# Fewer dummies, scale groups moved into half-done K steps, and spread layer-norm halves at the head of a DiT block

## The chip, the cores and the metric

The kernel runs on one core of one Trainium2 chip. The metric is the device time of one execution in microseconds (us), as the median of several runs. Besides, one execution per kernel is profiled; its span is about 1.8 us shorter than the time of the same run (245.3 against 247.12 for the kernel before), so spans are compared with spans and times with times.

A difference of 2% is the bar for "faster" or "slower".

## The reference

A diffusion-transformer block over x of 2 x 256 x 1152 in bf16. Only its start matters:

```python
mod = (_silu(c) @ w_mod).reshape(B, 6, 1, D)          # six modulation vectors per batch
shift_a, scale_a, gate_a, shift_m, scale_m, gate_m = [mod[:, i] for i in range(6)]
h = _layernorm(x, axis=-1) * (1 + scale_a) + shift_a
qkv = (h @ wqkv).reshape(B, N, 3, H, Dh)
# ... attention, wo, second modulated layer norm, two MLP matmuls with gelu
```

The kernel computes K before the shift is there: it multiplies the scaled norm (without shift) into w_k. (It may: a shift of k that is the same for all keys of a batch adds to each query's scores a constant, which softmax removes.)

## The kernel before

The parts that the change touches, with cuts marked. TensorE is PE here.

```python
def warm(n, dst):                       # fp32 dummies on zeros; one is two passes of 256 columns
    for _ in range(n):
        nc.tensor.matmul(dst[:, 0:T // 2], zeros32[:, 0:P], zeros32, start=True, stop=True)
# ... two dummies, transposition of c, silu, then:

def norm1(t, c0, c1):                   # VectorE: normalize columns c0..c1 of token tile t
    nc.vector.tensor_scalar(xns[t][:, c0:c1], x_sb[:, t, c0:c1], mv1[:, t, 0:1], rstd1[:, t:t + 1],
                            op0=ALU.subtract, op1=ALU.mult)

SGROUPS = [(0, 2), (2, 4), (4, 6), (6, 8), (8, 9)]
def scale_group(g):                     # 9 tiny matmuls (2 columns) per chunk; the add is returned
    k0, k1 = SGROUPS[g]
    pm = aux_tile([P, k1 - k0, B], "pm")
    for j in range(k0, k1):
        for k in range(KD):
            nc.tensor.matmul(pm[:, j - k0, :], w_scale_a[:, k, j * P:(j + 1) * P], sT[:, k, 0:B], ...)
    return lambda: nc.vector.tensor_scalar_add(scale_a[:, k0:k1, :], pm[:], 1.0)

def transpose_x(ks, ts): ...            # PE transposes chunks of xns into one PSUM tile pt

def modulate(pt, i, k, b, j0, eng):     # scale while copying out of PSUM, one batch at a time
    dst, src, sc = hT0[:, k, b * N:(b + 1) * N], pt[:, i, j0:j0 + N], scale_a[:, k, b:b + 1]
    if eng == "d": nc.vector.tensor_scalar_mul(dst, src, sc)
    else:          nc.scalar.mul(dst, src, sc)

def k_step(k, c0=0, c1=T):              # K chunk k into six PSUM accumulators
    for m in range(KM1):
        ...
        nc.tensor.matmul(pk[m][:, c0:c1], w_k[:, k, m * P:(m + 1) * P], hT0[:, k, c0:c1], ...)

def both(pt, k):                        # batch 0 on VectorE, batch 1 on ScalarE, same PSUM tile
    for b, e in enumerate("da"):
        modulate(pt, 0, k, b, b * N, e)

warm(13, pwarm)
# ... layer-norm statistics and first-half norms of the four tiles, scale group 0, k_steps 0 and 1 ...
modulate(pt_b, 0, 2, 0, 0, "d")
modulate(pt_b, 1, 3, 0, 0, "a")
for t in range(NT):                     # second-half norms, four in a row
    norm1(t, CUT, D)
k_step(1, N, T)
pt_d = transpose_x([2, 3], BT[1])
modulate(pt_d, 0, 2, 1, 0, "d")
modulate(pt_d, 1, 3, 1, 0, "a")
k_step(2, 0, N)
k_step(2, N, T)
scale_group(2)()
pt = transpose_x([4], range(NT))
both(pt, 4)
k_step(3)
pt = transpose_x([5], range(NT))
both(pt, 5)
k_step(4)
scale_group(3)()
# ... and so on to k_step(8), then three k panels, q, attention, MLP ...
```

Weights come over one DMA queue in the order of use: x, scale group 0, w_k rows 0 and 1, scale group 1, w_k rows 2 and 3, and so on.

Of the kernel before, what the change touches and what calls it, by code (L numbers as in the profile page):

```python
# [19 lines left out]
def kernel(  # L20
# [12 lines left out]
    B, N, D = x.shape  # L33
# [4 lines left out]
    T = B * N  # L38
    NT = T // P
# [20 lines left out]
    def acc_tile(shape, name, dt=FP32):  # L60
        return psum.tile(shape, dt, name=name, tag="acc", bufs=6)

    def aux_tile(shape, name, dt=FP32):
        return psum.tile(shape, dt, name=name, tag="aux", bufs=2)
# [34 lines left out]
    KM1 = 6  # L99
# [55 lines left out]
    pwarm = acc_tile([P, T], "pwarm")  # L155
# [4 lines left out]
    def warm(n, dst):  # L160
        for _ in range(n):
            nc.tensor.matmul(dst[:, 0:T // 2], zeros32[:, 0:P], zeros32, start=True, stop=True)  # L162
# [48 lines left out]
    def norm1(t, c0, c1):  # L211
        nc.vector.tensor_scalar(  # L212
            xns[t][:, c0:c1], x_sb[:, t, c0:c1], mv1[:, t, 0:1], rstd1[:, t:t + 1],
            op0=ALU.subtract, op1=ALU.mult,
        )
# [4 lines left out]
    def scale_group(g):  # L220
# [4 lines that stand above are left out]
                nc.tensor.matmul(  # L225
                    pm[:, j - k0, :], w_scale_a[:, k, j * P:(j + 1) * P], sT[:, k, 0:B],
                    start=(k == 0), stop=(k == KD - 1),
                )
        return lambda: nc.vector.tensor_scalar_add(scale_a[:, k0:k1, :], pm[:], 1.0)

    def transpose_x(ks, ts):
        pt = aux_tile([P, len(ks), len(ts) * P], "pt", BF16)
        for i, k in enumerate(ks):
            for j, t in enumerate(ts):
                nc.tensor.transpose(pt[:, i, j * P:(j + 1) * P], xns[t][:, k * P:(k + 1) * P], ident[:])  # L235
        return pt

    def modulate(pt, i, k, b, j0, eng):
        dst, src, sc = hT0[:, k, b * N:(b + 1) * N], pt[:, i, j0:j0 + N], scale_a[:, k, b:b + 1]
        if eng == "d":  # L240
            nc.vector.tensor_scalar_mul(dst, src, sc)  # L241
        else:
            nc.scalar.mul(dst, src, sc)

    pk = [None] * KD

    def k_step(k, c0=0, c1=T):
        for m in range(KM1):
            if k == 0 and c0 == 0:
                pk[m] = acc_tile([P, T], "pk")  # L250
            nc.tensor.matmul(  # L251
                pk[m][:, c0:c1], w_k[:, k, m * P:(m + 1) * P], hT0[:, k, c0:c1],
                start=(k == 0 and c0 == 0), stop=(k == KD - 1), skip_group_check=True,
            )
# [30 lines left out]
    CUT = 4 * P  # L285
    BT = [range(b * TPB, (b + 1) * TPB) for b in range(B)]

    def both(pt, k):
        for b, e in enumerate("da"):
            modulate(pt, 0, k, b, b * N, e)  # L290

    warm(13, pwarm)
    for j in range(NPD):
        stats_piece(0, j)
    sqrt1(0)
# [14 lines left out]
    add = scale_group(0)  # L310
# [8 lines left out]
    recip1(3)  # L319
    norm1(3, 0, CUT)  # L320
    k_step(0, 0, N)
    k_step(1, 0, N)
    pt_c = transpose_x([0, 1], BT[1])
    modulate(pt_c, 0, 0, 1, 0, "d")
    modulate(pt_c, 1, 1, 1, 0, "a")
    add = scale_group(1)
    k_step(0, N, T)
    pt_b = transpose_x([2, 3], BT[0])
    add()
    modulate(pt_b, 0, 2, 0, 0, "d")  # L330
    modulate(pt_b, 1, 3, 0, 0, "a")
    for t in range(NT):
        norm1(t, CUT, D)
    k_step(1, N, T)
    pt_d = transpose_x([2, 3], BT[1])
    modulate(pt_d, 0, 2, 1, 0, "d")
    modulate(pt_d, 1, 3, 1, 0, "a")
    k_step(2, 0, N)
    k_step(2, N, T)
    scale_group(2)()  # L340
    pt = transpose_x([4], range(NT))
    both(pt, 4)
    k_step(3)
    pt = transpose_x([5], range(NT))
    both(pt, 5)
    k_step(4)
    scale_group(3)()
    pt = transpose_x([6], range(NT))
    both(pt, 6)
    k_step(5)  # L350
    pt = transpose_x([7], range(NT))
    both(pt, 7)
    k_step(6)
    scale_group(4)()
    pt = transpose_x([8], range(NT))
    both(pt, 8)
    k_step(7)
    k_step(8)
    for m in range(KM1):
        k_evac(m)  # L360
# [344 lines left out]
    for b in range(B):  # L705
        for stepped in (True, False):
# [3 lines left out]
            for m, k in steps:  # L710
                m0 = m - m % 2
# [94 lines left out]
```

## Time and profile before

| kernel before | |
|---|---|
| time, median of the first 3 runs | 246.26 us (246.14 to 246.86) |
| span of the profiled execution (that run: 247.12 us) | 245.3 us |
| PE busy | 239.3 us, 98% |
| dummies end, first w_scale_a matmul | 11.04 us |
| k panels start | 28.42 us |

The chain that ended last, shares by engine, from the page of the kernel before:

```profile
PE 97%; DVE 1%; ACT 0%; issue 0%; DVEq 0%
```

So time is won only where PE itself waits or does work nobody needs. Both are found in the first 28 us. The timeline of PE shows the head; columns are start, length, engine, line, operation, tiles, shapes, count, and in brackets the idle time before and what ended it. Kernel before:

```profile
1.19 2.08 PE L162 MATMUL pwarm<-zeros 128*128 128x256 f32 x4 [1.19 <-DVE eps_t L93]
3.20 0.19 PE L165 MATMUL pc<-ident,c_sb 18*128 18x18 bf16 x1
3.32 7.88 PE L162 MATMUL pwarm<-zeros 128*128 128x256 f32 x26
11.04 0.59 PE L225 MATMUL pm<-sT,w_scale_a 128*128 128x2 bf16 x18
...
17.75 0.81 PE L251 MATMUL pk<-big,w_k 128*128 128x256 bf16 x6 [0.59 <-DVE big L241]
...
18.86 0.38 PE L235 MATMUL pt<-ident,xn 128*128 128x128 bf16 x4
19.08 1.46 PE L251 MATMUL pk<-big,w_k 128*128 128x512 bf16 x6
20.37 0.39 PE L235 MATMUL pt<-ident,xn 128*128 128x128 bf16 x4
20.60 1.46 PE L251 MATMUL pk<-big,w_k 128*128 128x512 bf16 x6
...
28.42 4.05 PE L280 MATMUL pk<-big,w_k 128*128 128x512 bf16 x18
```

A record is longer than the distance to the next start (512 columns: 0.379 us against 0.216; I call the excess the drain), so work is read from start to start: a k_step of 512 columns takes 20.37 - 19.08 = 1.29 us. The dummies run without a break to 11.04 us. After the dummies, the idle 0.59 us at 17.75 is the only wait of PE for VectorE (0.75 us from start to start). Its cause is in VectorE's timeline of the kernel before: four norms in a row ahead of the modulation that k_step 2 needs.

```profile
15.93 1.51 DVE L212 TENSOR_SCALAR xn<-x_sb,mv,rstd 128x640 bf16<-128x640 bf16 x4
17.36 0.34 DVE L241 TENSOR_SCALAR big<-pt,scale_a 128x256 bf16<-128x256 bf16 x1
```

One more line, from the table of waits before (us in total, times, longest): ScalarE's modulations wait for VectorE's modulation of the same PSUM tile, eight times.

```profile
ACT big L243 <- DVE big L241: 10.2, 8, 1.6
```

No ScalarE modulation overlaps its VectorE partner: each of the eight starts 0.03 to 0.04 us after the partner has ended (19.30 + 0.35 = 19.65, then 19.69).

Not in a page view, but in the single records of the trace: the dummies' passes (26 of them for the thirteen dummies) start every 0.427 us up to 7.3 us and every 0.216 us after. The clock record puts the change at 7.42 us. I call this the opening of the gate, and the rates before and after the half and the full or open clock.

### The profile page before, as it was taken

The page shows a single profiled execution, that of the slowest core. Times are in us where ns is not written, and L with a number is a line of the kernel's source. Part 1 is how long each engine was busy: PE and PEld are TensorE (multiplying, and loading weights), DVE is VectorE, ACT ScalarE, POOL GpSimd, SP SyncE. Part 2 cuts the span into 40 slices and gives each one's busy share as a digit, 9 for nine tenths or more (in the row PEclk, how much of TensorE's full clock was granted, in tenths as well). Part 3 has the DMA queues.
Part 4 walks back from the last instruction along what each step waited for, and adds up shares of the span by engine and source line. Part 5 has one row for each costly group of instructions (what it writes and reads, how often), then busy time and mean ns, then how long its engine had stood idle before and what let it go on. Part 6 is the DMA issues. An engine that isn't in the chain of part 4 may idle for free.

```text
span 245.3 us, 3997 instructions
## 1 busy us (share of the span) xinstructions
PE 239.3 (98%) x1708; PEld 147.0 (60%) x1708; DVE 92.9 (38%) x200; ACT 61.4 (25%) x119; POOL 25.4 (10%) x37
## 2 busy tenths in 40 slices
PE   8989999999999999999999999999999999999993
PEld 5776444457667656788854444444566556655673
DVE  4662452324614578933000999970010000000001
ACT  6432432225414321564333222332000000000000
POOL 1000000022000222200000000001112211111111
PEclk9999999999999999999999999999999999999999
DMA  6999999993679997248999999199630000000000
GB/s 214 328 315 326 379 370 392 390 391 136 167 234 397 390 377 116 48 90 276 391 391 391 351 327 319 25 332 329 202 105 19 17 16 16 19 17 30 20 16 16
DMA packets 48780, 53.28 MB, mean 217 GB/s; under 512 B 9587, under 2 KB 36475, under 8 KB 48763
## 3 DMA queue, kind: packets, MB, share of 16 engines
q1 hardware_dynamic: 41312, 50.14, 61.1%
q10 hardware_dynamic: 6939, 1.71, 4.3%
q0 software_dynamic: 512, 1.19, 1.6%
q8 instruction: 13, 0.21, 0.4%
q14 instruction: 4, 0.03, 0.0%
HBM read 50.14 MB, written 1.19 MB: 209 GB/s over the span
## 4 chain that ended last, share of the span: by engine, by line
PE 97%; DVE 1%; ACT 0%; issue 0%; DVEq 0%
PE pacc L695 29%; PE pacc L751 29%; PE pacc L641 7%; PE pq L472 7%; PE pacc L551 7%; PE pk L251 4%; PE pwarm L162 4%; PE pk L280 2%; PE pa L589 2%; PE ps_s L509 2%; PE pn L370 2%; PE pm L225 1%; PE pt L235 1%; DVE xn L212 1%; PE pg L452 0%; DVE big L241 0%
## 5 line engine op out<-in xcount | busy, mean ns | idle before, releaser
L695 PE MATMUL pacc<-hT,w_f 128*128 128x256 bf16 (+1 forms) x432 | 70.5, 326 | 0.0
L751 PE MATMUL pacc<-w_f,gT 128*128 128x384 bf16 (+2 forms) x468 | 70.5, 314 | 0.0
L751 PEld LDWEIGHTS <-gT 128*128 128x128 bf16 x468 | 44.3, 98 | 26.3
L695 PEld LDWEIGHTS <-w_f 128*128 128x128 bf16 x432 | 42.1, 98 | 27.7
L757 DVE TENSOR_TENSOR tmp<-pacc,gate 128x384 f32<-128x384 f32 (+2 forms) x13 | 6.9, 527 | 65.6 <-PE pacc L751 55.1
L727 ACT ACTIVATE gT<-pacc 128x512 bf16<-128x512 f32 x24 | 14.3, 597 | 32.7 <-PE pacc L695 32.7
L423 DVE SCALAR_TENSOR_TENSOR part<-w_gate_m,s,part 128x1152 f32<-128x1152 bf16 x16 | 21.4, 1414 | 0.0
L641 PE MATMUL pacc<-w_o,big 128*128 128x384 bf16 x108 | 18.1, 326 | 0.0
L472 PE MATMUL pq<-hT,w_q 128*128 128x512 bf16 x81 | 18.0, 380 | 0.0
L551 PE MATMUL pacc<-w_v,hT 128*128 128x384 bf16 x108 | 17.7, 326 | 0.0
L759 POOL TENSOR_TENSOR o_sb<-tmp,x 128x384 bf16<-128x384 f32 (+1 forms) x12 | 11.6, 970 | 51.9 <-DVE tmp L757 51.9
L551 PEld LDWEIGHTS <-hT 128*128 128x128 bf16 x108 | 10.5, 98 | 7.1 <-issue 0.2
L641 PEld LDWEIGHTS <-big 128*128 128x128 bf16 x108 | 10.3, 98 | 7.3 <-issue 0.7
L251 PE MATMUL pk<-big,w_k 128*128 128x256 bf16 (+1 forms) x72 | 13.3, 326 | 1.2 <-DVE big L241 0.6
L472 PEld LDWEIGHTS <-w_q 128*128 128x128 bf16 x81 | 7.8, 98 | 9.4 <-issue 0.3
L162 PE MATMUL pwarm<-zeros 128*128 128x256 f32 x30 | 10.0, 502 | 1.2 <-DVE eps_t L93 1.2
L647 POOL TENSOR_TENSOR x<-tmp,x_sb 128x384 f32<-128x384 f32 x8 | 7.3, 913 | 34.2 <-DVE tmp L646 34.2
L421 DVE TENSOR_SCALAR part<-w_gate_m,s 128x1152 f32<-128x1152 bf16 x2 | 1.5, 817 | 22.2 <-DMA w_gate_m<-in_w_mod_dram 22.2
L251 PEld LDWEIGHTS <-w_k 128*128 128x128 bf16 x72 | 6.7, 97 | 4.9 <-issue 1.5
L162 PEld LDWEIGHTS pwarm<-zeros 128*128 128x128 f32 x30 | 7.5, 257 | 2.6 <-DVE eps_t L93 1.2
L716 ACT ACTIVATE gT<-pacc 128x512 bf16<-128x512 f32 x12 | 6.5, 598 | 8.8 <-PE pacc L695 8.8
L445 POOL DMA_DIRECT2D gates_dram<-nat_v x2 | 1.1, 531 | 67.5 <-DVE nat_v L443 67.5
(91 smaller groups left out, 161.4 us busy)
## 6 DMA issues: line engine op xcount, KB each, us to landing
w_f<-in_w_fc_dram SPq DMA_DIRECT2D x12, 864.0 KB, 14.8
w_f<-in_w_fc_dram SPq DMA_DIRECT2D x3, 1728.0 KB, 8.1
w_f<-in_w_fc_dram SPq DMA_DIRECT2D x2, 2592.0 KB, 18.2
w_gate_a<-in_w_mod_dram SPq DMA_DIRECT2D x3, 864.0 KB, 12.0
w_v<-in_wqkv_dram SPq DMA_DIRECT2D x3, 864.0 KB, 14.1
w_o<-in_wo_dram SPq DMA_DIRECT2D x3, 864.0 KB, 14.3
w_shift_m<-in_w_mod_dram SPq DMA_DIRECT2D x3, 864.0 KB, 6.5
w_scale_m<-in_w_mod_dram SPq DMA_DIRECT2D x3, 864.0 KB, 12.1
```

The lines of the kernel that those rows point to most:

```text
L162: nc.tensor.matmul(dst[:, 0:T // 2], zeros32[:, 0:P], zeros32, start=True, stop=True)
L251: nc.tensor.matmul(pk[m][:, c0:c1], w_k[:, k, m * P:(m + 1) * P], hT0[:, k, c0:c1], start=(k == 0 and c0 == 0), stop=(k == KD - 1), skip_g ...
L423: nc.vector.scalar_tensor_tensor(part[:, b, :], wg[:, k, :], s32[:, k, b:b + 1], part[:, b, :], op0=ALU.mult, op1=ALU.add,)
L472: nc.tensor.matmul(pq[m][:], w_q[:, k, m * P:(m + 1) * P], hT[:, k, :], start=(k == 0), stop=(k == KD - 1), skip_group_check=True,)
L551: nc.tensor.matmul(pacc[:], hT[:, k, t * P:(t + 1) * P], w_v[:, k, pnl * PW:(pnl + 1) * PW], start=(k == 0), stop=(k == KD - 1),)
L641: nc.tensor.matmul(pacc[:], aT[:, k, t * P:(t + 1) * P], w_o[:, k, c0:c1], start=(k == 0), stop=(k == KD - 1),)
L647: (nc.gpsimd if pool_add else nc.vector).tensor_tensor(x1[:, t, c0:c1], tmp[:], x_sb[:, t, c0:c1], op=ALU.add)
L695: nc.tensor.matmul(dst, w_f1[m // KD][:, k, ml * P:(ml + 1) * P], hT[:, k, c0:c1], start=start, stop=(k == KD - 1), **kw,)
L727: nc.scalar.activation(gT[:, m, :], pacc[:], ACT.Gelu_apprx_tanh)
L751: nc.tensor.matmul(pacc[:], gT[:, kk, t * P:(t + 1) * P], w_f2[j][:, r, c0 - n * PW:c0 - n * PW + cw], start=(kk == 0), stop=(kk == KF - 1),)
L757: nc.vector.tensor_tensor(tmp[:], pacc[:], gate_m[:, b, c0:c0 + cw], op=ALU.mult)
L759: (nc.vector if last else nc.gpsimd).tensor_tensor(o_sb[:], tmp[:], x1[:, t, c0:c0 + cw], op=ALU.add)
```

## The change

Three edits, meant to start the real work sooner and to keep PE fed. Four dummies go; scale groups 2, 3 and 4 each move between two halves of a K step, so that PE has work around it; the second-half norms are spread between the modulations.

```diff
-    def k_step(k, c0=0, c1=T):
-        for m in range(KM1):
+    def k_step(k, c0=0, c1=T, m0=0, m1=KM1):
+        for m in range(m0, m1):
...
-    warm(13, pwarm)
+    warm(9, pwarm)
...
     modulate(pt_c, 1, 1, 1, 0, "a")
+    norm1(0, CUT, D)
     add = scale_group(1)
...
-    for t in range(NT):
-        norm1(t, CUT, D)
+    norm1(1, CUT, D)
     k_step(1, N, T)
...
     modulate(pt_d, 1, 3, 1, 0, "a")
+    norm1(2, CUT, D)
+    norm1(3, CUT, D)
     k_step(2, 0, N)
     k_step(2, N, T)
-    scale_group(2)()
+    k_step(3, 0, T, 0, 3)
+    add = scale_group(2)
     pt = transpose_x([4], range(NT))
+    add()
     both(pt, 4)
-    k_step(3)
+    k_step(3, 0, T, 3, KM1)
...  (the same for scale groups 3 and 4 inside k_steps 5 and 7)
```

More of the change, by code (lines that the diff above doesn't have):

```diff
@@ L346 @@
     k_step(4)
-    scale_group(3)()
+    k_step(5, 0, T, 0, 3)
+    add = scale_group(3)
     pt = transpose_x([6], range(NT))
+    add()
     both(pt, 6)
-    k_step(5)
+    k_step(5, 0, T, 3, KM1)
     pt = transpose_x([7], range(NT))
@@ L353 @@
     k_step(6)
-    scale_group(4)()
+    k_step(7, 0, T, 0, 3)
+    add = scale_group(4)
     pt = transpose_x([8], range(NT))
+    add()
     both(pt, 8)
-    k_step(7)
+    k_step(7, 0, T, 3, KM1)
     k_step(8)
```

## The prediction

> **What bounds it now.** TensorE: the chain of waits gives PE 97% of the 245.3 us span, the table of engines 98% busy. After about 18 us the PE has no idle stretch before any large group, so only the head can change; what follows should shift as a block (DMA issues after 30 us wait for PE progress; w_shift_a, w_q and w_v land over 3 us before use).
>
> **The head, from the timeline of PE.** fp32 dummies run to 11.04 us. Each dummy is two passes. Passes start every 0.427 us up to 7.32 us and every 0.216 us after. [...] Then: scale group 0 (0.45), first modulations (k_step starts 12.45), steps to 28.42, where the k panels begin. Idle worth naming: 0.75 us before the second half of k_step 2 (17.0 to 17.75), because VectorE does four second-half norms in a row (1.51 us) ahead of a modulation.
>
> **The change, term by term.**
> 1. Four dummies fewer: eight passes, at the open-clock rate: 8 x 0.216 = 1.73 us, dummies would end at 9.31. But the first w_scale_a group lands (last of its 16 engines) at 9.43; the second VectorE norm it also needs ends at 9.40. So scale group 0 starts at about 9.5 instead of 11.04: -1.5 us. The DMA queues are full here (share above 1.0), so data come no earlier.
> 2. Norms spread: the 0.75 us wait disappears: -0.75 us. Later loads stay just in time: scale group 1 lands 12.5, wanted 12.5; rows 2-3 of w_k 13.6, wanted 14.9; group 2 15.6, wanted 16.8.
> 3. Half steps: no work added, but less PE work lies between a transposition and the step that reads it. From first transposition to ScalarE's modulation finished takes 1.34 us in the timeline (18.86 to 20.20): VectorE 0.35, then ScalarE 0.47, which starts only after VectorE (8 waits, 10.2 us in the table of waits[...]). Before, 1.74 us of PE work covered it; now 0.22+0.65+0.22 = 1.09. New gaps: about 0.25 before k_step 4, 0.25 before 6, 0.47 before 8 (0.87 covered): +0.97 us.
>
> Sum for the profiled execution: -1.5 - 0.75 + 0.97 = -1.3 us, k panels at about 27.1.
>
> **The timed runs.** If the gate's phase varies from run to run, [...] while after always starts at the landing, 9.5. The before runs spread over 0.72 us, which fits. Then the average gain of term 1 is nearer 1.0 us and the total about 0.8 to 1.0. I predict 245.3 us (-0.4%), 80% range 244.5 to 246.2. Faster by over 2%: 1%; within 2%: 98%; slower: 1%. After should also vary less than before.
>
> **What would show it.** Term 1: first w_scale_a matmul at 9.4 to 9.7 us, waiting for its DMA or just after the dummies. Term 2: no PE idle from VectorE's norms before k_step 2; 128x640 norms no longer four in a row. Term 3: PE idle released by ScalarE modulations before k_step 4, 6 and 8, about 0.25, 0.25 and 0.5 us. Start of the k panels at 27.1; everything after unchanged in length.
>
> **What would make it wrong.** The gate closing again [...] (head matmuls at twice the spacing) [...]. DMA landings of group 1 or w_k later than the trace of before. The gaps of term 3 not appearing would give 244.3; gate phase always early would leave gain near zero.

The sum for the profiled execution is -1.5 - 0.75 + 0.97 = -1.3 us. For the timed runs term 1 shrank from -1.5 to about -1.0 us and the sum to -1.0 - 0.75 + 0.97 = -0.8 (0.8 to 1.0), which gave the forecast of 245.3 us. The gate's phase is the time of its opening.

## The result, and the profile after

| | before | changed |
|---|---|---|
| time, median of 4 runs | 246.31 us (246.14 to 246.86) | 245.72 us (245.46 to 245.81) |
| ratio | | 0.9971, 95% interval 0.9953 to 0.9988 |
| span of the profiled execution | 245.3 us | 244.0 us |
| first w_scale_a matmul | 11.04 us | 9.41 us |
| k panels start | 28.42 us | 27.08 us |

Ratios and intervals here and below are worked out from the fast runs alone and are not quite the ratio of the medians quoted. Executions over 1.5% slower than the fastest of the same kernel are left out of the means.

The chain by engine, from the page of the changed kernel:

```profile
PE 96%; DVE 1%; ACT 1%; issue 1%; DVEq 0%
```

Timeline of PE, changed kernel:

```profile
3.32 6.08 PE L162 MATMUL pwarm<-zeros 128*128 128x256 f32 x18
9.41 0.60 PE L225 MATMUL pm<-sT,w_scale_a 128*128 128x2 bf16 x18
...
14.75 2.12 PE L251 MATMUL pk<-big,w_k 128*128 128x256 bf16 x14
16.70 0.59 PE L225 MATMUL pm<-sT,w_scale_a 128*128 128x2 bf16 x18
17.16 0.38 PE L235 MATMUL pt<-ident,xn 128*128 128x128 bf16 x4
17.38 0.81 PE L251 MATMUL pk<-big,w_k 128*128 128x512 bf16 x3
18.02 0.39 PE L235 MATMUL pt<-ident,xn 128*128 128x128 bf16 x4
18.51 2.10 PE L251 MATMUL pk<-big,w_k 128*128 128x512 bf16 x9
...
21.77 0.39 PE L235 MATMUL pt<-ident,xn 128*128 128x128 bf16 x4
22.27 2.10 PE L251 MATMUL pk<-big,w_k 128*128 128x512 bf16 x9
...
24.65 0.81 PE L251 MATMUL pk<-big,w_k 128*128 128x512 bf16 x3
25.79 1.45 PE L251 MATMUL pk<-big,w_k 128*128 128x512 bf16 x6 [0.32 <-ACT big L243]
27.08 4.05 PE L280 MATMUL pk<-big,w_k 128*128 128x512 bf16 x17
```

Three things are to be seen. The first scale group starts at 9.41 us, where its load has just landed (9.36; this and the other landings below are from the single records of the traces, which no view prints). The VectorE wait before the second half of k_step 2 is gone: the line at 14.75 runs through. And there are new holes: the transpositions at 18.02 take 0.22 from start to start, yet the next k_step starts at 18.51, 0.27 us late; before k_step 8 the hole is 0.49 us (24.65 + 3 x 0.216 = 25.30, start 25.79), of which the view shows 0.32, as it counts the drain of the matmul before as busy. The third, before k_step 6, is 0.28 (22.27 - 21.77 - 0.22).

VectorE's timeline has the norms in three places now:

```profile
12.83 0.44 DVE L212 TENSOR_SCALAR xn<-x_sb,mv,rstd 128x640 bf16<-128x640 bf16 x1
...
14.34 0.44 DVE L212 TENSOR_SCALAR xn<-x_sb,mv,rstd 128x640 bf16<-128x640 bf16 x1
14.95 0.35 DVE L241 TENSOR_SCALAR big<-pt,scale_a 128x256 bf16<-128x256 bf16 x1 [0.18 <-PE pt L235]
15.22 0.79 DVE L212 TENSOR_SCALAR xn<-x_sb,mv,rstd 128x640 bf16<-128x640 bf16 x2
```

And the wait of ScalarE for VectorE, in the table of waits of the changed kernel:

```profile
ACT big L243 <- DVE big L241: 10.6, 8, 2.4
```

Everything later is the kernel before, moved: the k panels, the first MLP matmul (100.65 against 99.31) and the second (171.21 against 169.87) all start 1.34 us earlier. In the two profiled executions, then, the change is -1.3 us and fully accounted for. The timed runs show about half of that. That difference is what the experiments are about.

### The profile page after: what moved, and what is told of

It is laid out like the page before. It is cut to its first block, busy times and chain, and to the rows that moved or that the text cites. A ratio compares the mean times of both kernels' runs of the same rounds, so it can differ in the third digit from the quotient of the medians.

```text
span 244.0 us, 3970 instructions
## 1 busy us (share of the span) xinstructions
PE 237.4 (97%) x1689; PEld 145.5 (60%) x1700; DVE 92.9 (38%) x200; ACT 61.5 (25%) x119; POOL 25.4 (10%) x37
## 4 chain that ended last, share of the span: by engine, by line
PE 96%; DVE 1%; ACT 1%; issue 1%; DVEq 0%
PE pacc L759 29%; PE pacc L703 29%; PE pacc L649 7%; PE pq L480 7%; PE pacc L559 7%; PE pk L251 4%; PE pwarm L162 3%; PE pk L280 2%; PE pa L597 2%; PE ps_s L517 2%; PE pn L378 2%; PE pm L225 1%; ACT big L243 1%; PE pg L460 0%; PE pt L235 0%
## 5 line engine op out<-in xcount | busy, mean ns | idle before, releaser
L162 PE MATMUL pwarm<-zeros 128*128 128x256 f32 x22 | 8.2, 541 | 1.2 <-DVE eps_t L93 1.2
L654 DVE TENSOR_TENSOR tmp<-pacc,gate 128x384 f32<-128x384 f32 x12 | 6.6, 552 | 3.7 <-PE pacc L649 3.7
```

## The experiments

**The theory.** (A) Three independent terms, -1.5, -0.75 and +0.97 us. The first depends on the opening of the gate: it comes at a time that varies from run to run, dummies therefore end at varying times in the kernel before, and the profiled execution of before was one where it opened late. **The rival.** (B) The gate opens at the same time in all runs, and the timed gain is smaller because something later in the kernel gives time back.

Twelve runs were made, in three batches, each compared with runs of the kernel before on the same chip; three of them repeat an earlier kernel, and one the kernel before. For the third batch (e9 to e12) eleven of the twelve runs of before are those of the second batch, 8 minutes earlier. All kernels were correct.

### e1: the dummies alone

```diff
-    warm(13, pwarm)
+    warm(9, pwarm)
```

> The kernel before with nine dummies instead of thirteen, nothing else changed. Theory A (the profile of before caught a late opening of the clock gate; on the timed runs the gate opens at other times, and the first scale group is then bound by its load, which lands at 9.4 us): in the trace the first w_scale_a matmul starts at 9.4 to 9.6 us, the 0.75 us wait for the four norms before the second half of k_step 2 stays, the k panels start at about 26.9 us; timed gain over before only about 0.9 us (ratio 0.9963). Rival B (the gate always opens near 7.3 us, and the shortfall of the timed gain comes from elsewhere, later in the kernel): timed gain 1.5 us (ratio 0.994).

Measured: 245.99 us (246.95, 246.87, 245.48, 245.58, 245.91, 246.07), before 246.70; ratio 0.9977, interval 0.9954 to 0.9999. The first scale group started at 9.25 us, just after its load (9.20) and 0.15 us before the expected range, but the k panels started only at 28.26 and not at 26.9. The gate had opened at 5.21 us in this execution (7.42 in the first one of before: it does vary), the dummies were over early, and then the clock fell to half again, from 12.04 to 15.45 us. The halved stretch lasted 3.41 us and began 6.83 us, twice that, after the opening; in e8 below it is 3.41 and 6.83 again. So I cut the time from the opening on into stretches of 3.41 us and call them windows; whether the chip counts in such windows was not shown. The first three of e1, by the windows view; columns are the stretch, its length, busy time (instructions) of PE, weight loads, VectorE, ScalarE and GpSimd, then the granted clock, the DMA share and GB/s:

```profile
5.21:8.62 3.41, 3.18 (x15) 2.46 (x13) 3.00 (x9) 2.46 (x5) 0.00 (x0) 1.00 1.00 302
8.62:12.04 3.41, 2.07 (x32) 1.71 (x33) 2.66 (x13) 2.07 (x7) 0.00 (x0) 1.00 1.14 321
12.04:15.45 3.41, 3.41 (x37) 2.77 (x36) 0.60 (x3) 0.47 (x1) 0.00 (x0) 0.50 1.14 322
```

The clock column reads 0.50 in the last. From the first scale group to the k panels took 19.01 us here, against 17.38 in the first trace of before: 1.6 us lost. The prediction has such a second closing only in its list of what would make it wrong. This became the second question: when does it happen, and does the changed kernel pay it?

### e2: the norms alone

```diff
+    norm1(0, CUT, D)          # after the modulations of pt_c
...
-    for t in range(NT):
-        norm1(t, CUT, D)
+    norm1(1, CUT, D)
...
+    norm1(2, CUT, D)          # after the modulations of pt_d
+    norm1(3, CUT, D)
```

> The kernel before with only the second-half norms spread. Both theories: the PE wait of 0.75 us before the second half of k_step 2 disappears and nothing else moves: -0.75 us (ratio 0.9970), and that in every run, whatever the gate did, since it comes after the dummies. If the wait is only passed on to another engine (ScalarE behind VectorE), the gain is under 0.4 us.

Measured: 245.99 us (245.38 to 246.44), before 246.70; ratio 0.9969 (0.9950 to 0.9988), that is -0.76 us. In its trace k_step 2 runs through, and from the first scale group (11.03) to the k panels (27.65) it takes 16.62 us instead of 17.38: -0.76. The term is confirmed in both. The two lines, in the timeline of e2:

```profile
11.03 0.59 PE L225 MATMUL pm<-sT,w_scale_a 128*128 128x2 bf16 x18
...
27.65 4.05 PE L280 MATMUL pk<-big,w_k 128*128 128x512 bf16 x18
```

### e3: the half steps alone

```diff
-    scale_group(2)()
+    k_step(3, 0, T, 0, 3)
+    add = scale_group(2)
     pt = transpose_x([4], range(NT))
+    add()
     both(pt, 4)
-    k_step(3)
+    k_step(3, 0, T, 3, KM1)
...  (the same for groups 3 and 4)
```

> The kernel before with only the scale groups put inside half-done K steps. My reading: slower by 0.8 to 1.0 us (ratio 1.0035 to 1.004), with PE idle of about 0.27, 0.28 and 0.49 us before k_steps 4, 6 and 8, released by ScalarE's modulations. Rival (the half steps hide the wait for the scale group and pay for themselves): same or faster, by up to 0.5 us.

Measured: 247.47 us (246.94 to 248.29), before 246.70; ratio 1.0026 (1.0007 to 1.0045), +0.64 us. In its trace the stretch from first scale group (11.21) to k panels (29.60) is 18.39 us, 1.01 more than before. In the timeline of e3, the two ends of the stretch and the gap before k_step 8:

```profile
11.21 0.59 PE L225 MATMUL pm<-sT,w_scale_a 128*128 128x2 bf16 x18
...
28.31 1.46 PE L251 MATMUL pk<-big,w_k 128*128 128x512 bf16 x6 [0.32 <-ACT big L243]
29.60 4.05 PE L280 MATMUL pk<-big,w_k 128*128 128x512 bf16 x17
```

The trace gives the expected size; the timed value is smaller than expected, though 0.8 to 1.0 lies in its interval. Either way the half steps cost time, and the rival, that they pay for themselves, is out for these conditions.

### e4: the changed kernel without the half steps

Edit: e1 and e2 together.

> The changed kernel with the whole K steps of before (nine dummies, norms spread). My reading: the three PE waits before k_steps 4, 6 and 8 vanish, the k panels start at about 26.15 us instead of 27.08, span about 243.1; timed about 1.6 us under before (ratio 0.9935), 0.95 us under the changed kernel. Loads stay ahead: scale groups 2 and 3 land at 15.6 and 18.6 us, wanted at 16.2 and 19.6. Rival (half steps needed because the earlier PE would otherwise wait for the loads of scale groups): PE waits for w_scale_a before groups 2 to 4, and the time equals the changed kernel's 245.7.

Measured: 244.60 us in four runs (244.5 to 244.9), before 246.70; ratio 0.9916 (0.9898 to 0.9935). The k panels start at 25.95 us and the span is 242.9; the gaps are gone and none of the scale groups 2 to 4 waits for its load in this trace. The gain over before, 2.1 us, is larger than the expected 1.6; e10 below shows that part of it was luck.

### e5: both modulations on VectorE

```diff
-        for b, e in enumerate("da"):
+        for b, e in enumerate("dd"):
```

> The changed kernel, with the modulations of K chunks 4 to 8 of both batches on VectorE instead of one on VectorE and one on ScalarE. If the three new waits of the half steps are the serial pair VectorE 0.35 then ScalarE 0.47 us, two VectorE instructions in a row (they start 0.27 us apart) shorten the pair by 0.24 us: the waits before k_steps 4 and 6 (0.27 and 0.28 us) vanish, the one before k_step 8 falls from 0.49 to about 0.25, gain about 0.8 us over the changed kernel, k panels at about 26.3 us in a trace with the same clock. Rival (the waits come from the scale group's own chain, matmul to add to modulation, which this leaves alone): gain under 0.3 us.

Measured: 245.28 us. Its profiled run (253.32 us, mean granted clock 0.95) does not count; the other five were 244.94, 244.98, 245.19, 245.37 and 246.41. Before was 246.16; ratio 0.9965 (0.9941 to 0.9990). Repeated as e11.

### e6: six dummies

```diff
-    warm(9, pwarm)          # of e4
+    warm(6, pwarm)
```

> The kernel without half steps (e4) with six dummies instead of nine; the first scale group is bound by its load at 9.2 to 9.4 us either way. Theory (a 3.41 us window in which the PE is idle for over a third halves the clock in the next, as in the trace of e1): the PE idles about 1.8 us before the first scale group, the window after the opening is then mostly idle, and the clock halves for 3.4 us somewhere between 8.6 and 15 us in most runs: 0.9 to 1.7 us slower than e4's 244.6, so 245.5 to 246.3, with a stretch of clock 0.5 in the trace. Rival (the half clock in e1 was chance, nothing to do with idle time): 244.6, clock 1.0 after the opening.

Measured: 244.52, 244.39, 245.98, 247.76, 244.56, 246.34; median 245.27, ratio 0.9974 (0.9934 to 1.0015). Half the runs lie at 244.4 to 244.6 and half 1.4 to 3.4 us above, where I had expected most of them up to 1.7 above. The traced run is one of the good ones: the gate opened at 5.19, PE waited 2.1 us for the load, and the clock stayed full. So the theory as I had put it was too simple: PE idle for over a third of a window (it was busy 1.89 of 3.41 us in the window from 5.19) did not close the gate. Windows view of e6:

```profile
5.19:8.60 3.41, 1.89 (x9) 1.34 (x7) 3.25 (x10) 3.14 (x7) 0.00 (x0) 1.00 1.02 301
8.60:12.02 3.41, 2.25 (x36) 1.99 (x37) 2.48 (x11) 1.42 (x5) 0.00 (x0) 1.00 1.13 330
```

### e7: a dummy in the wait for ScalarE

```diff
     pt_a = transpose_x([0, 1], BT[0])     # in e4
+    warm(1, pwarm)
```

> The kernel without half steps (e4) with one more dummy (two passes, 0.43 us at the open clock) between the first transpositions and k_step 0, where the PE otherwise waits 0.56 us for ScalarE. It should cost nothing: median 244.6 as e4, within 0.2 us; and as it adds PE work to the window most at risk of being too idle, no run should be over 245.3. Rival: it delays k_step 0 and costs 0.2 to 0.4 us.

Measured: 245.43, 244.83, 246.03, 244.71, 245.14, 244.92; median 245.03, ratio 0.9957 (0.9936 to 0.9979). The dummy fits into the gap (k_step 0 starts 0.96 us after the transpositions, as in e4). The bound of 245.3 failed twice. One of the two has a trace, and its cause is another: scale group 3 landed at 20.13 us and not at about 18.5, and PE waited 0.50 us for it. This is what a half step can hide: in the changed kernel's trace that group is wanted only at 20.45, in e4 at 19.43. In the other traces it landed between 17.6 and 19.0, and once, in the slow one, at 20.3. The run at 246.03 has no trace, but the record gives the mean granted clock of every run, and this one's is 0.991, like that of the traced halvings (0.991 in e1, 0.993 in e8). By that figure the clock fell to half in it too, and the added dummy did not prevent that.

### e8: the changed kernel again

No edit.

> The changed kernel once more, unchanged, beside the others on the same chip. From its first runs: median 245.7, ratio to before 0.997; if the gate opens early (near 5.2 us) in some run, the clock may halve again near 8.6 to 12 us and that run will be near 246.5. Its trace gives one more opening time of the gate, to compare with 7.2 to 7.8 us in five traces and 5.2 us in one.

Measured: 247.37, 245.67, 247.24, 245.81, 245.51, 245.83; median 245.82, before 246.16; ratio 0.9991 (0.9965 to 1.0018). The traced run is the one at 247.37: the gate opened at 4.68 us, the dummies were over at about 8.1, PE waited 1.5 us for a load that landed late (9.62), and the clock was halved from 11.50 to 14.92 us. Windows view of e8:

```profile
4.68:8.09 3.41, 3.41 (x16) 2.66 (x14) 3.24 (x10) 3.10 (x6) 0.00 (x0) 1.00 0.92 257
8.09:11.50 3.41, 1.30 (x27) 1.11 (x27) 2.56 (x12) 1.88 (x7) 0.00 (x0) 1.00 1.14 326
11.50:14.92 3.41, 3.41 (x36) 2.66 (x35) 1.37 (x6) 0.56 (x2) 0.00 (x0) 0.50 1.15 320
```

From first scale group to k panels it took 19.01 us, against 17.67 in the first trace of the changed kernel: 1.34 us. So the changed kernel does pay for the second halving in some runs, here in two of six: the other slow run, 247.24, has no trace but a mean granted clock of 0.990. Both are above the 246.5 expected of such a run.

### e9: dummies paced by data

```diff
-    warm(9, pwarm)          # of e4
+    warm(7, pwarm)
...
     act_stats(ACT.Square, dsq)
+    for _ in range(4):
+        nc.tensor.matmul(pwarm[:], ident[:], xns[T_ACT][:, 0:T], start=True, stop=True)
```

> The kernel without half steps (e4) with seven dummies, and then four bf16 dummies of 512 columns (0.86 us together) that read what ScalarE's second statistics pass writes, so that they cannot start before 8.3 to 8.4 us whatever the clock gate did. Theory (the half clock after an early opening comes from a 3.41 us window with too little matmul work, 37% and 19% in the two traces that show it, at least 47% in all windows that were followed by a full clock): with an opening at 4.7 or 5.2 us the window at risk now holds about 0.56, the clock stays full, and all runs lie between 244.3 and 245.1, with one allowed up to 245.6 when scale group 3 lands late (near 20 us). Rival (the halving does not depend on this work): a third of the runs at 246 or more, as in e1, e6 and e8.

Measured: 244.71, 244.94, 244.78, 244.76, 244.97, 245.63; median 244.86, before 246.22; ratio 0.9951 (0.9930 to 0.9972). All six lie in the expected range and its one exception at the edge. The traced run opened late (7.52), so the trace does not show the case that the edit is for; the paced dummies start at 8.50 us there and end where the first scale group starts, at 9.37. The load had landed at 8.32 in this execution, so here they cost something: k_step 0 started at 10.78, where e10 (below), with a landing at 8.65, reached it at 10.31.

### e10: e4 again

No edit to e4.

> The kernel without half steps (e4) once more, unchanged. Its four runs were 244.5 to 244.9, which by the theory was luck: it has the same nine dummies as the changed kernel, so early openings of the gate should now and then halve its clock again. Expected: median 244.6 to 244.9, one or two of six runs at 245.8 to 246.6. Rival: all six below 245.1, the half steps being what provokes the second halving.

Measured: 244.20, 244.67, 244.58, 246.03, 245.96, 246.22; median 245.32, before 246.22; ratio 0.9961 (0.9932 to 0.9991). Three of six runs are 1.3 us and more above the others. Their mean granted clocks are 0.991 and 0.992, those of the others 1.0. One or two such runs were expected, and a median of 244.9 at most. So the four even runs of e4 were luck, and the half steps are not what provokes the loss.

The granted clocks settle more than the times do. In the batches of these experiments and in the first runs of the changed kernel, 14 runs of the state fast have 0.985 to 0.993, each above every other run of its kernel in time; all others have 0.997 or more. With nine dummies (the paced ones of e9 apart) they are 11 of 43, with six 3 of 6, with thirteen none of 37. So it is the removal of dummies that lets the clock halve again.

The trace is of the run at 244.20, and it makes a pair with e8: the gate opened at 4.71 us, 0.03 later than there, and up to this point the kernels issue the same PE work. But the load landed at 8.65 instead of 9.62, the first scale group began almost 1 us earlier, and the clock stayed full. Windows view of e10:

```profile
4.71:8.12 3.41, 3.41 (x16) 2.66 (x14) 3.31 (x10) 3.21 (x6) 0.00 (x0) 1.00 0.99 295
8.12:11.54 3.41, 2.27 (x35) 1.86 (x35) 2.83 (x13) 1.70 (x7) 0.00 (x0) 1.00 1.10 336
11.54:14.95 3.41, 3.41 (x52) 3.11 (x50) 2.03 (x7) 1.11 (x3) 0.00 (x0) 1.00 1.14 323
```

The windows at 8.6 (e1) and 8.1 us (e8) had 2.07 and 1.30 us of PE and were followed by half a clock; those of e10 and e6 (8.60 to 12.02) had 2.27 and 2.25 and were not. These busy times include the drain of the last matmul. With that taken off (0.166 us from each record, an estimate from 0.379 us of a record less 0.216 us between starts, rounded up), the share of matmul work is 37% and 18% in the two that closed, 42% and 47% in e10 and e6. But e6's window before that had 1.89 us of PE (50% by the estimate) and stayed open too, so busy time with the drain does not order the windows. The estimate does, but only because it counts the 2-column matmuls of the scale groups (records of 0.163 us) as no work at all: counted at the 0.025 us between their starts, they bring e1's window, which closed, to 51%, the same as e6's earlier one, which did not. Of all full-clock windows in the heads of the traces, e10's 42% is the lowest that was not followed by half a clock. As a few matmul records can be missing from a trace (the page of the changed kernel has 1689, with 1700 weight loads), these shares are rough, and they give no threshold.

### e11: e5 again

No edit to e5.

> The changed kernel with chunks 4 to 8 modulated by VectorE alone, once more, because the profile of e5 fell in a slow state. Wanted: a trace at full clock that shows the waits before k_steps 4, 6 and 8 (0.27, 0.28, 0.49 us in the changed kernel) as 0, 0 and about 0.25. Time of the runs without a second halving near 245.1, between 244.9 (all three waits gone) and 245.8 (none).

Measured: 245.16, 244.79, 245.11, 246.37, 244.87, 246.47; median 245.14, before 246.22; ratio 0.9969 (0.9942 to 0.9996). The trace is at full clock. PE and VectorE, around k_steps 3 and 4, in the timeline of e11:

```profile
17.53 0.81 PE L251 MATMUL pk<-big,w_k 128*128 128x512 bf16 x3
17.76 0.61 DVE L241 TENSOR_SCALAR big<-pt,scale_a 128x256 bf16<-128x256 bf16 x2
18.18 0.39 PE L235 MATMUL pt<-ident,xn 128*128 128x128 bf16 x4
18.42 2.10 PE L251 MATMUL pk<-big,w_k 128*128 128x512 bf16 x9
```

The pair of modulations takes 0.61 us instead of 0.86, and k_step 4 starts 0.24 us after the transpositions, 0.02 late at most. Before k_step 6 it is the same (21.68 to 21.92). Before k_step 8 a gap of 0.24 us is left in the single records (last matmul of k_step 7 at 24.74, next at 25.19). Expected were 0, 0 and 0.25. So the new waits of the changed kernel are the serial pair VectorE, then ScalarE, and not the chain of the scale group. From first scale group to k panels it took 16.90 us, 0.77 less than in the changed kernel's first trace. Without the halved runs, the four of e11 average 244.98 us and the four of e8 245.71.

### e12: the kernel before again

No edit.

> The kernel before, unchanged, for one more trace with thirteen dummies. Theory: the first w_scale_a matmul starts at 11.04 - 0.49 x (7.42 - opening), the opening being that of this trace (7.42 in the first; 0.49 us because a pass takes 0.427 us at the half clock and 0.216 at the full one), and the span is 245.3 less the same amount, within 0.3 us. The clock is not halved again even after an opening near 5 us, as thirteen dummies last to 9.8 us at least. Rival (start of the scale group fixed): 11.0 us whatever the opening.

Measured: 246.37 us, span 244.6. The gate opened at 5.91 us. The formula gives 11.04 - 0.49 x 1.51 = 10.30. Timeline of PE in e12:

```profile
3.32 7.14 PE L162 MATMUL pwarm<-zeros 128*128 128x256 f32 x26
10.29 0.59 PE L225 MATMUL pm<-sT,w_scale_a 128*128 128x2 bf16 x18
```

10.29, and the span is 0.7 us shorter for it. No second halving. Together with the other traces (e6 and e9, with other dummies, left out):

| trace | dummies | gate opens | load of group 0 landed | first scale group | half clock again |
|---|---|---|---|---|---|
| before | 15 | 7.42 | 9.43 | 11.04 | no |
| e2 | 15 | 7.40 | 8.87 | 11.03 | no |
| e3 | 15 | 7.76 | 9.54 | 11.21 | no |
| e12 | 15 | 5.91 | 9.28 | 10.29 | no |
| changed | 11 | 7.26 | 9.36 | 9.41 | no |
| e4 | 11 | 7.10 | 9.27 | 9.32 | no |
| e7 | 11 | 6.37 | 9.32 | 9.37 | no |
| e11 | 11 | 5.77 | 9.54 | 9.59 | no |
| e1 | 11 | 5.21 | 9.20 | 9.25 | 12.04 to 15.45 |
| e10 | 11 | 4.71 | 8.65 | 8.70 | no |
| e8 | 11 | 4.68 | 9.62 | 9.66 | 11.50 to 14.92 |

(Dummies include the two before c arrives.) With the four more, the start follows the gate and not the load; with four fewer it follows the load by 0.04 to 0.05 us, whatever the gate did. That settles A against B as to the gate: its opening varies, and the start of before with it.

## Why the prediction was right or wrong

The range, 244.5 to 246.2 us around 245.3, holds the measured 245.72, and "within 2%" came true. The gain came out at 0.59 us by the medians (0.7 by the ratio), a little short of the 0.8 to 1.0 predicted; in the second set of runs (e8) the ratio leaves 0.2. That the first set came so near was partly luck: none of its four runs was halved (granted clocks 0.998 to 1.0), while two of the six of e8 were.

1. **Dummies.** Predicted start of the first scale group 9.4 to 9.7 us, bound by the load and not by the dummies: 9.41, landing 9.36. Right; in the other traces with nine dummies it was 9.25 to 9.66, and 8.70 in e10, always just after the landing. The saving is 1.6 us when the gate opens at 7.4 and 1.0 us when it opens at 5.9, where e12 put the dummies' end at 10.29 and the load came at 9.28. That the profiled execution of before was a late one was inferred from its spread alone; e12 showed it.
2. **Norms.** Predicted -0.75 us; e2 measured -0.76 in its trace and in its ratio. Right.
3. **Half steps.** Predicted gaps of 0.25, 0.25 and 0.47; the trace has 0.27, 0.28 and 0.49, and 1.01 us in all in e3. The cause, VectorE then ScalarE on one PSUM tile, was confirmed by e11, where one engine does both and 0.02, 0.02 and 0.24 are left. The timed cost in e3 was 0.64 with a wide interval.
4. **The rest of the kernel moves as a block.** Right: 1.34 us at each milestone.
5. **"After should also vary less than before".** True of the first four runs (0.35 us against 0.72), false of the next six (1.86 us). The step that failed here is the one that let the start of the scale group decide alone ("after always starts at the landing"). It does start there; but when the gate opens early, the dummies end up to 1.5 us before the landing, and in some of these runs (e1, e8) the clock halves again for 3.4 us. That it is the little matmul work in the window before that does it is argued from e1, e8 and e10, not shown. A second closing was listed as what would make the prediction wrong; it measured 1.6 us in e1 and 1.3 in e8. Two of the ten runs of the changed kernel were at 247.2 to 247.4 against 245.5 to 245.8 for the other eight, and one of the two is traced. An extra 1.6 us in two runs of ten is 0.3 us on the average: a good part of what the predicted gain has over the measured ratios. The rest may be noise: without the two, e8 is 0.54 us under the mean of before, and the interval of the first ratio, 0.3 to 1.2 us, holds the predicted gain.

What stays open: the exact rule of the second halving (the estimate of 37% against 42% rests on two windows closed and on one way of counting). The untraced slow runs of e1, e5, e6, e7, e8, e10 and e11 are halvings by their granted clocks, but in which window they fell is not known. A late load of a scale group, as in e7, costs up to 0.5 us there too. What sets the time of the opening (4.68 to 7.76 us in thirteen traces of state fast) is not known, nor what sets that of the first group's landing (8.32 to 9.62).

The experiments point to a better kernel: nine dummies' worth of work, the last part tied to data, spread norms, whole K steps (e9). It ran at 244.86 us, 1.36 below the kernel before by the medians, and 0.96 below the changed kernel's 245.82 on the same chip a few minutes earlier. Its advantage over plain e4 is evenness (no run over 245.7 in six and no granted clock under 0.997, against three halved runs in e10), but six runs are few, none of them is known to have opened early, and at the rate of 11 in 43 six even runs in a row would still come about one time in six.

## What to carry to other kernels

Dummy work ahead of the first real matmuls should end when the first real data arrive, and as the moment of opening varies from run to run (4.68 to 7.76 us here), its length in instructions is the wrong measure: tying the last part to an event that varies less (VectorE's first step after ScalarE's second pass started at 8.34 to 8.79 us in seven traces) is what e9 tries, with the promise and the doubt given above. Before moving work into a gap, count how much of it stands between a producer and its consumer elsewhere: half a step moved forward uncovered a 1.34 us chain that a whole step had hidden. And a profile is one draw: compare the span of the profiled run with the spread of the timed ones before costing a difference from it.
